# Wider fill matmuls, gated second halves and gated loads in a fused Sinkhorn-attention and bilinear FFN kernel

## The chip, the cores and the metric

The kernel runs on one core of a Trainium2 chip. The metric is the device time of one execution in microseconds (us); for the kernel before, it is the median of 11 runs. The engines are named TensorE (PE in the profile, its weight loads PEld), VectorE (DVE), ScalarE (ACT), GpSimd (POOL) and SyncE (SP). In this kernel POOL issues all loads from DRAM (they cast fp32 to bf16 on the way), and SP issues everything else: DMA transposes, a round trip of v through DRAM, and the stores.

## The reference

Inputs are q, k, v of shape (4, 8, 768, 64), a sort matrix of 8x8 for each batch and head, and three weights.

```python
P = sort_net
for _ in range(5):
    P = P - np.max(P, axis=-1, keepdims=True)
    P = np.exp(P)
    P = P / (np.sum(P, axis=-1, keepdims=True) + 1e-09)
    P = P / (np.sum(P, axis=-2, keepdims=True) + 1e-09)
k_sorted = np.einsum('bhij,bhjcd->bhicd', P, k_b).reshape(B, H, S, D)
v_sorted = np.einsum('bhij,bhjcd->bhicd', P, v_b).reshape(B, H, S, D)
...
scores = scale * np.matmul(q_b, k_sb.transpose(0, 1, 2, 4, 3))
...
attn = attn / (np.sum(attn, axis=-1, keepdims=True) + 1e-09)
return np.matmul(attn, v_sb).reshape(B, H, S, D).astype(np.float32)
```

The keys and values of the 8 blocks (96 tokens each) are mixed by P, each block of queries attends to its own mixed block, and the result x, as 3072 tokens of 512, goes through `(x @ w_a) * (x @ w_b) @ w_out` with 1536 hidden columns.

## The kernel before

**Tiling and stages.** The four batches are worked in order; the 8 heads of a batch are four pairs p, and a pair's 8 blocks are two halves h of four. One unit of attention is (b, p, h): the mixing matmuls of k and v with the spread P (L496 for batch 0, where each half is mixed by itself; L485 and L533 later), a transpose of v (L555, not for batches 2 and 3), scores (L574), exp on ACT (L579), the product with v (L589), and on DVE a reciprocal and a multiplication into xp (L595, L600; the operation `o_mul`). Then x is transposed into xT: batch 0 by TensorE (L608) and a copy, later batches by a DMA transpose on SP (`x_dma`, L616). q is transposed by TensorE for batches 0 and 1 (L469) and by a DMA transpose on SP for batches 2 and 3 (`q_dma`, L621; `QDMA`, L194). For batches 2 and 3 v goes through DRAM and comes back in another layout (`v_out` L542, `v_back` L546).

After a batch's attention come the two FFN stages. Batch 0 has plain products (`ab_plain`, L743; half t of the tokens needs xT of all four pairs' half h = t). Batches 1 to 3 use a Strassen scheme (`ab_strassen`, L825) on sums that `x_sums` and `w_sums` make (L306, which is the line of every two-operand elementwise operation). In it each column group g has two chains of 14 matmuls; ACT takes snapshots (L834), DVE adds (a and f), and DVE or POOL multiplies the two results into hT. `out_plain` (L893) does the last product; the attention of batch b+2 is mixed into `out_plain` of batch b.

**What sets the order.** No loop order is written out. Each piece of work is an `Op` with an engine (or alternatives with a duration each), a duration in the plan's own us, what it depends on (`deps`), which buffers it takes and gives back (`get`, `put`), and a rank. `Plan.solve` (L132) runs a list schedule: at each step it takes the operation that can start earliest, the lowest rank among those that can start within a small margin, on the engine that ends it first. Every engine and every DMA queue then runs its instructions in the order of the planned starts, so an instruction that waits holds up all behind it on its engine. Latencies after an operation are `LAT` or the `lat` given.

**Loads.** `load` (L311) puts an issue of 0.72 on POOL and a transfer on a planned DMA queue. A load waits for the one seven before it (`ld_n[-7]`), and for its buffer: the rings k2, v2 and q2 have 6 buffers each, for 16 pairs in all. `load_pair` (L394) loads k, v and q of a pair; for batches 2 and 3 q is loaded by `q_wide` (L350) in two DMAs. The loads of batches 2 and 3 are added one after the other at L941 to L943 with ranks 30 to 43, with no dependency other than buffers and the seven.

**Batch 0.** L921 to L927 add the first halves of the four pairs at ranks 0 to 3, L929 to L935 the second halves at ranks 10 to 25, which depend only on their loads and buffers. `ab_plain` of batch 0 has ranks from 10.

**Fill.** While TensorE has nothing to do in the first 32.6 planned us (`warm_until`, L973), `_fill` (L177) adds matmuls whose result nobody reads, so that TensorE is not idle. `warm` (L967) writes them to a PSUM bank of their own, n matmuls of 128 columns per planned gap:

```python
unit = 0.056 if t > 4.0 else 0.08
n = int((o.start - t - 0.05) / unit)
```

Of the kernel before, what the change touches and what calls it, by code (L numbers as in the profile page):

```python
# [35 lines left out]
class Plan:  # L36
# [12 lines left out]
    def add(self, eng, dur, fn, deps=(), get=(), put=(), rank=0.0, lat=None):  # L49
        alts = dict(eng) if isinstance(eng, (list, tuple)) else {eng: dur}  # L50
        op = Op(alts, fn, deps, list(get), list(put), rank, lat, len(self.ops))
        for key in op.put:
            self.holders[key] = self.holders.get(key, 0) + 1
        self.ops.append(op)
        return op
# [121 lines left out]
    def _fill(self):  # L177

        t, ops = self.warm_from, sorted((o for o in self.ops if o.eng == "PE"), key=lambda o: o.start)
        for o in ops:  # L180
            if o.start > self.warm_until:
                break
            unit = 0.056 if t > 4.0 else 0.08
            n = int((o.start - t - 0.05) / unit)
            if n > 1:
                w = Op({"PE": 0.0}, lambda n=n: self.warm_fn(n), [], [], [], 0.0, None, -1)
                w.eng, w.start, w.end = "PE", t, t + n * unit
                self.ops.append(w)
            t = max(t, o.end)

# [8 lines left out]
def kernel(  # L199
# [11 lines left out]
    nc = tc.nc  # L211
    P = 128
    B, H, S, D = q.shape
# [9 lines left out]
    HP = H // 2  # L223
# [16 lines left out]
    add = plan.add  # L240
# [3 lines left out]
    ps = [psp.tile([P, 2, 512], FP32, name=f"ps{n}") for n in range(4)]  # L244
# [64 lines left out]
    ld_n = []  # L309

    def load(fn, nbytes, deps=(), get=(), rank=0.0, many=0.0):  # L311
        ds = list(deps) + ([ld_n[-7]] if len(ld_n) >= 7 else [])
        i = add("POOL", 0.72 + many, fn, ds, get=get, rank=rank, lat=0.0)
        d = add("DQ", nbytes / 333e3, None, [i], rank=rank)
        ld_n.append(d)
        return d
# [33 lines left out]
    def q_wide(b, p):  # L350
        t = buf(("q2", b, p))
        for e in range(2):
            nc.gpsimd.dma_start(  # L353
                out=_ap(t, e * D, [[2 * W, P], [2 * D, NCH], [1, D]]),
                in_=_ap(q, (b * H + 2 * p + e) * S * D, [[W, P], [D, NCH], [1, D]]))

    def kv(b, p, name, t):
        nc.gpsimd.dma_start(  # L358
            out=buf((name, b, p)),
            in_=_ap(t, (b * H + 2 * p) * S * D, [[W, P], [S * D, 2], [1, W]]))  # L360
# [30 lines left out]
    for c in range(1, 4):  # L391
        load_ab(c)

    def load_pair(b, p, rank):  # L394
        for name, t, into in (("k2", k, k_in), ("v2", v, v_in)):
            into[b, p] = load(lambda name=name, t=t: kv(b, p, name, t), NB_KV,
                              get=[(name, (name, b, p))], rank=rank)
        if QDMA(b, p):
            q_in[b, p] = load(lambda: q_wide(b, p), NB_KV * 1.5,
                              get=[("q2", ("q2", b, p))], rank=rank, many=0.9)  # L400
        else:
            q_in[b, p] = load(lambda: nc.gpsimd.dma_start(
                out=buf(("q2", b, p)),
                in_=_ap(q, (b * H + 2 * p) * S * D, [[W, P], [S * D, 2], [1, W]])), NB_KV,
                get=[("q2", ("q2", b, p))], rank=rank)


    last = o_p
# [54 lines left out]
    def q_pe(b, p, h):  # L463
        q2, ps_ = buf(("q2", b, p)), buf(("qp", b, p, h)).bitcast(BF16)
        i0, n = (0, NB) if h is None else (h * NBH, NBH)
        p0, np_ = i0 * CG, n * CG
        for c in range(NCH):
            for e in range(2):
                nc.tensor.matmul(  # L469
                    ps_[e * D:(e + 1) * D, c * np_:(c + 1) * np_],  # L470
                    lhsT=_ap(q2, p0 * 2 * W + e * W + c * D, [[2 * W, np_], [1, D]]),
                    rhs=ident[p0:p0 + np_, p0:p0 + np_], is_transpose=True)
# [31 lines left out]
                           [[2 * HK, P], [CG, NCH], [BLK, NBH], [1, CG]]),  # L504
             _ap(buf((what + "m", b, p, h)), 0, [[1024, P], [n, NCH], [CG, NBH], [1, CG]]))

    def mix_half(b, p, what, h, rk):
        pe = add("PE", 0.3, lambda: mix_half_pe(b, p, what, h),
                 [(k_in if what == "k" else v_in)[b, p], s_ok[b, p]],
                 get=[("bank", (what + "m", b, p, h))], put=[(what + "2", b, p)], rank=rk)  # L510
        op = add((("ACT", 0.48), ("DVE", 0.56)), None, None,
                 [pe, o_pads, first.get((what + "T", b, p))],
                 get=[(what + "T", (what + "T", b, p))] if h == 0 else [],
                 put=[(what + "m", b, p, h)], rank=rk)
        first[what + "T", b, p] = op
        op.fn = lambda: mix_half_copy(op.eng, b, p, what, h)
        return op
# [97 lines left out]
    def x_dma(b, p):  # L615
        nc.sync.dma_start_transpose(  # L616
            out=_ap(buf(("xT", b)), p * S, [[KA * S, P], [BLK, NB], [1, BLK]]),
            in_=buf(("xp", b, p)).rearrange("q i e d -> q (i e d)"))

    def q_dma(b, p):  # L620
        nc.sync.dma_start_transpose(  # L621
            out=_ap(buf(("qT", b, p)), 0, [[NB * BLK, P], [P, NCH], [1, P]]),
            in_=buf(("q2", b, p)))
# [33 lines left out]

    first = {}

    def q_part(b, p, h, rk):  # L660
        if QDMA(b, p):
            return add("SP", 1.2, lambda: q_dma(b, p), [q_in[b, p]], get=[("qT", ("qT", b, p))],
                       put=[("q2", b, p)], rank=rk, lat=2.6)
        qi = q_in[b, p, h] if (b, p, h) in q_in else q_in[b, p]
        pe = add("PE", 0.38 if h is not None else 0.46, lambda: q_pe(b, p, h), [qi, o_ident],
                 get=[("bank", ("qp", b, p, h))], put=[("q2", b, p)], rank=rk)
        alts = (("ACT", 0.48),) if h == 0 else (("ACT", 0.48), ("DVE", 0.36)) if h == 1 else (
            ("ACT", 0.8), ("DVE", 0.55))
        op = add(alts, None, None, [pe, first.get(("q", b, p))],
                 get=[("qT", ("qT", b, p))] if h in (0, None) else [],  # L670
                 put=[("qp", b, p, h)], rank=rk)
        first["q", b, p] = op
        op.fn = lambda: q_copy(op.eng, b, p, h)
        return op
# [28 lines left out]
    def x_home(b):  # L703
        if ("xTgot", b) not in st:
            st["xTgot", b] = add("NIL", 0.0, None, get=[("xT", ("xT", b))], rank=-20)
        return st["xTgot", b]
# [9 lines left out]
    def attention(b, p, rk):  # L716
        qd = q_part(b, p, None, rk)
        ks, vs = mix_part(b, p, rk, False)
        if not VDMA(b, p):
            vs = [v_part(b, p, None, vs[0], rk)]  # L720
        ms = [so_part(b, p, h, False, ks[0], qd, vs[0], rk + 0.5 + 0.1 * h) for h in range(2)]
        d = add("SP", 1.2, lambda: x_dma(b, p), ms + [x_home(b)], put=[("xp", b, p)],
                rank=rk + 0.7, lat=2.6)
        for h in range(2):
            xT_done.setdefault((b, h), []).append(d)
# [195 lines left out]
    for p in range(HP):  # L921
        rk = float(p)
        qd = q_part(0, p, 0, rk)
        kd = mix_half(0, p, "k", 0, rk)
        vd = v_part(0, p, 0, mix_half(0, p, "v", 0, rk + 0.05), rk + 0.1)
        m = so_part(0, p, 0, True, kd, qd, vd, rk + 0.1)
        x_part(0, p, 0, m, rk + 0.15)  # L927
    R0 = 10.0
    for p in range(HP):  # L929
        rk = R0 + 5.0 * p  # L930
        qd = q_part(0, p, 1, rk)
        kd = mix_half(0, p, "k", 1, rk)
        vd = v_part(0, p, 1, mix_half(0, p, "v", 1, rk), rk + 1.0)
        m = so_part(0, p, 1, True, kd, qd, vd, rk + 1.0)
        x_part(0, p, 1, m, rk + 2.0)  # L935
    for p in range(HP):
# [1 line left out]
    later_spreads(5)  # L938
    for c in range(3):
        load_out(c, 20)  # L940
    for b in range(2, B):  # L941
        for p in range(HP):
            load_pair(b, p, 30 + 10 * (b - 2) + p)  # L943

    for t in range(2):
        for m in range(KO):
# [6 lines left out]
    for b in range(B):  # L953
        for t in range(2):
            for c in range(3):
                out_plain(b, t, c, RB + 40.0)
        if b + 1 == B:
            break
        if b + 2 < B:
            for p in range(HP):  # L960
                attention(b + 2, p, RB + 36.0 + 0.5 * p)
        tx_ok = x_sums(b + 1, RB + 49.0)
        for g in range(G):
            ab_strassen(b + 1, g, RB + 50.0 + 4 * g, ws_ok, tx_ok, out_last[b])
        RB += 100.0

    def warm(n):  # L967
        touched.add(7)
        for _ in range(n):
            nc.tensor.matmul(ps[3][:, 1, 0:P], lhsT=warm_sb[:, 0:P], rhs=warm_sb[:, 0:P],  # L970
                             start=True, stop=True)

    plan.warm_until, plan.warm_fn, plan.warm_from = 32.6, warm, 1.2  # L973
    order = plan.solve()
# [74 lines left out]
```

## Time and profile before

| what | value |
|---|---|
| median of 11 runs | 257.68 us (254.27 to 259.05) |
| the profiled execution's own time | 257.37 us |
| its span, first to last instruction | 255.6 us |
| mean granted TensorE clock | 0.963 of full |
| TensorE busy | 237.2 us (93%), 2322 matmuls, 2335 weight loads |
| VectorE, ScalarE, GpSimd busy | 158.0, 124.3, 100.6 us |
| software DMA queue (POOL's loads) | 29296 packets, 14.16 MB, 45.2% of 16 engines' span |
| hardware DMA queue (SP's) | 27312 packets, 13.38 MB, 27.1% |
| instruction queue | 18 packets, 0.29 MB |

How to read it: times are counted from the span's start. A row of slices cuts the span in 40 equal parts, and each digit is a busy share in tenths; PEclk is the TensorE clock that was granted. A wait is the idle time of an engine before an instruction, with what ended it; "issue" is idle time for which the profile shows nothing that was waited for. The chain of waits is followed back from the last instruction, at each step to what released it. A line L306 or L248 is a helper's, so such groups are told apart by their tiles.

### The profile page before, as it was taken

The numbers are of one execution on the slowest core, as the hardware profiler recorded it, in microseconds if no ns is written. First come the engines' busy times: TensorE is split into PE (matmuls) and PEld (weight loads), VectorE is DVE, ScalarE is ACT, GpSimd is POOL, SyncE is SP. The second block draws the span as 40 slices with busy tenths as digits, with TensorE's granted clock in tenths as the row PEclk, the third lists the DMA queues.
The fourth block names the chain that finished last, engine by engine and source line by source line (L and its number), as shares of the span: only waits on it lengthen the run. The fifth ranks groups of instructions, "written<-read, shape, count | busy, mean of one in ns | idle before, by whom it ended". The sixth has DMA issues, their size and how long they took to land.

```text
span 255.6 us, 5986 instructions
## 1 busy us (share of the span) xinstructions
PE 237.2 (93%) x2322; PEld 144.0 (56%) x2335; DVE 158.0 (62%) x363; ACT 124.3 (49%) x240; POOL 100.6 (39%) x122
## 2 busy tenths in 40 slices
PE   8987999999999943999999999999999999999992
PEld 7865875666665412455565445556564455655440
DVE  6664589945566305558897646678895329888120
ACT  3353645466765522246667543476661136765010
POOL 8879936843945700002434320044440002455000
PEclk9996599999999995999999999999999999999998
DMA  5999992999999999974003476310024451000135
GB/s 75 170 201 188 204 201 37 170 191 193 161 148 184 166 123 190 253 169 92 0 1 61 95 181 165 80 44 0 0 43 83 94 121 35 1 0 3 41 82 123
DMA packets 56636, 27.91 MB, mean 109 GB/s; under 512 B 36641, under 2 KB 53537, under 8 KB 56609
## 3 DMA queue, kind: packets, MB, share of 16 engines
q0 software_dynamic: 29296, 14.16, 45.2%
q1 hardware_dynamic: 27312, 13.38, 27.1%
q8 instruction: 18, 0.29, 0.5%
q14 instruction: 10, 0.07, 0.1%
HBM read 29.89 MB, written 7.86 MB: 148 GB/s over the span
## 4 chain that ended last, share of the span: by engine, by line
PE 86%; DMA 7%; issue 2%; POOL 2%; ACT 1%; DVE 1%; DVEq 0%
PE ps L825 32%; PE ps L893 23%; PE ps L743 12%; DMA qT<-q 5%; PE ps L589 4%; PE ps L574 3%; PE ps L485 3%; DMA q<-in_q_dram 2%; PE ps L555 2%; PE ps L496 2%; PE ps L970 2%; PE ps L469 2%; PE ps L533 1%; PE ps L608 1%; POOL k L358 1%
## 5 line engine op out<-in xcount | busy, mean ns | idle before, releaser
L306 POOL TENSOR_TENSOR hT<-a,f 128x384 bf16<-128x384 bf16 x39 | 35.5, 917 | 107.1 <-DVE f L306 104.0
L893 PE MATMUL ps<-w_out_sb,hT 128*128 128x512 bf16 x275 | 64.2, 380 | 1.1 <-issue 0.7
L834 ACT COPY f<-ps 128x384 f32<-128x384 f32 x108 | 48.2, 482 | 21.4 <-PE ps L825 18.0
L893 PEld LDWEIGHTS <-hT 128*128 128x128 bf16 x288 | 27.3, 98 | 30.9 <-issue 0.5
L579 ACT ACTIVATE eT<-ps 96x768 bf16<-96x768 f32 x32 | 25.1, 805 | 30.0 <-PE ps L574 29.6
L306 DVE TENSOR_TENSOR f<-f,ps 128x384 f32<-128x384 f32 x54 | 29.2, 549 | 7.4 <-PE ps L825 5.3
L306 DVE TENSOR_TENSOR a<-f,ps 128x384 bf16<-128x384 f32 x54 | 29.6, 549 | 5.2 <-ACT f L834 3.7
L306 DVE TENSOR_TENSOR hT<-a,ps 128x384 bf16<-128x384 bf16 x42 | 23.0, 547 | 6.5 <-PE ps L743 3.4
L248 ACT COPY o<-ps 128x512 f32<-128x512 f32 x13 | 7.5, 585 | 36.5 <-PE ps L893 33.7
L825 PE MATMUL ps<-tx,ws_b 128*128 128x384 bf16 x108 | 24.9, 326 | 0.0
L825 PE MATMUL ps<-tx,ws_a 128*128 128x384 bf16 x108 | 24.0, 326 | 0.0
L600 DVE TENSOR_TENSOR xp<-ps,rec 96x512 bf16<-96x512 f32 x32 | 21.6, 682 | 0.4
L250 DVE COPY o<-ps 128x512 f32<-128x512 f32 x11 | 7.6, 687 | 20.3 <-PE ps L893 20.2
L743 PE MATMUL ps<-xT,w_a_sb 128*128 128x384 bf16 x96 | 19.6, 326 | 0.0
L743 PE MATMUL ps<-xT,w_b_sb 128*128 128x384 bf16 x96 | 19.6, 326 | 0.0
L825 PEld LDWEIGHTS <-ws_b 128*128 128x128 bf16 x144 | 14.1, 98 | 9.4
L825 PEld LDWEIGHTS <-ws_a 128*128 128x128 bf16 x144 | 13.6, 98 | 10.0 <-ACT f L834 0.6
L749 ACT CAST a<-ps 128x384 bf16<-128x384 f32 x24 | 11.4, 477 | 14.2 <-PE ps L743 11.7
L574 PE MATMUL ps<-qT,kT 64*128 64x96 bf16 x256 | 10.4, 213 | 7.8 <-DMA qT<-q 7.7
L825 PE MATMUL ps<-xT,w_a_sb 128*128 128x384 bf16 x72 | 17.6, 326 | 0.0
L825 PE MATMUL ps<-xT,w_b_sb 128*128 128x384 bf16 x72 | 17.6, 326 | 0.0
L353 POOL DMA_DIRECT2D q<-in_q_dram x16 | 13.2, 830 | 5.9 <-DMA k<-in_k_dram 2.7
(92 smaller groups left out, 338.7 us busy)
## 6 DMA issues: line engine op xcount, KB each, us to landing
out_dram<-o SPq DMA_DIRECT2D x48, 128.0 KB, 2.4
k<-in_k_dram POOLq DMA_DIRECT2D x16, 192.0 KB, 6.7
v<-in_v_dram POOLq DMA_DIRECT2D x16, 192.0 KB, 7.2
q<-in_q_dram POOLq DMA_DIRECT2D x24, 96.0 KB, 8.3
w_a_sb<-in_moe_w_a_dram POOLq DMA_DIRECT2D x4, 384.0 KB, 7.8
w_b_sb<-in_moe_w_b_dram POOLq DMA_DIRECT2D x4, 384.0 KB, 9.5
w_out_sb<-in_moe_w_out_dram POOLq DMA_DIRECT2D x3, 512.0 KB, 11.2
vd<-vm SPq DMA_DIRECT2D x8, 192.0 KB, 2.8
```

The source lines that it names most:

```text
L306: ENG[eng].tensor_tensor(out=out, in0=in0, in1=in1, op=op)
L353: nc.gpsimd.dma_start(out=_ap(t, e * D, [[2 * W, P], [2 * D, NCH], [1, D]]), in_=_ap(q, (b * H + 2 * p + e) * S * D, [[W, P], [D, NCH], [1 ...
L485: nc.tensor.matmul(mix[e * D:(e + 1) * D, c // 4, c % 4 * P:(c % 4 + 1) * P], lhsT=src[:, e, c * D:(c + 1) * D], rhs=s_all[:, b * H + 2 * ...
L574: nc.tensor.matmul(sc[:, e, i * BLK:(i + 1) * BLK], lhsT=kT[e * D:(e + 1) * D, at:at + P], rhs=rhs, start=True, stop=True)
L579: nc.scalar.activation(out=buf(("eT", b, p, h))[:, :, 0:HB], in_=buf(("sc", b, p, h))[0:BLK, :, 0:HB], func=AF.Exp, scale=float(scale))
L589: nc.tensor.matmul(ops_[:, e, i * OW:(i + 1) * OW], lhsT=eT[:, e, i * BLK:i * BLK + P], rhs=vs[:, h * NBH + i, e * OW:(e + 1) * OW], start ...
L600: nc.vector.tensor_tensor(out=_ap(xp, h * NBH * 2 * D, [[NB * 2 * D, BLK], [D, 2], [2 * D, NBH], [1, D]]), in0=_ap(ops_, 2, [[1024, BLK], ...
L743: nc.tensor.matmul(pf[:, 0:HW], lhsT=w_sb[:, kc, m * P:(m + 1) * P], rhs=buf(("xT", b))[:, kc, t * HW:(t + 1) * HW], start=(kc == 0), stop ...
L749: ea = add("ACT", 0.48, lambda: nc.scalar.copy(out=buf(("a", b, t, m)), in_=buf(("pf", b, t, m, "a"))[:, 0:HW]), [pa], get=[("a", ("a", b, ...
L825: nc.tensor.matmul(buf(key)[:, 0:HW], lhsT=lf(j), rhs=rf(j), start=start and j == 0, stop=j == 1, skip_group_check=not start)
L834: return add("ACT", 0.48, lambda: nc.scalar.copy(out=buf((name, b, g, n)), in_=buf(kA)[:, 0:HW]), [dep], get=[("f", (name, b, g, n))], rank=r)
L893: nc.tensor.matmul(po, lhsT=hT[:, t * 2 + m // G, m % G, c * P:(c + 1) * P], rhs=w_out_sb[:, m, :], start=(m == 0), stop=(m == KO - 1), sk ...
```

## The change

It has four parts.

1. Fill: the gap is counted in columns, not matmuls, and `warm` makes matmuls of 512 columns and one rest of at least 32. Up to 5 planned us the rate is 1180 columns per us, later 2350. They write the whole of the same PSUM bank.
2. Batch 0: the q, k and v matmuls of a pair's second half get a dependency on the `o_mul` of the same pair's first half (`st["gate", p]`).
3. Loads: only batch 2 is loaded where batches 2 and 3 were. The loads of batch 3 are added after the attention of batch 2, at ranks 40 to 43, and each k, v and q load depends on `o_mul` of batch 2, pair 2, second half (`st["last", 2, 2]`).
4. Plan: `q_dma` counts 1.3 us with 3.2 until it has landed (before 1.2 and 2.6), `x_dma` 1.5 (before 1.2).

```diff
-            unit = 0.056 if t > 4.0 else 0.08
-            n = int((o.start - t - 0.05) / unit)
-            if n > 1:
-                w = Op({"PE": 0.0}, lambda n=n: self.warm_fn(n), [], [], [], 0.0, None, -1)
-                w.eng, w.start, w.end = "PE", t, t + n * unit
+            rate = 2350.0 if t > 5.0 else 1180.0
+            cols = int((o.start - t - 0.06) * rate)
+            if cols >= 64:
+                w = Op({"PE": 0.0}, lambda cols=cols: self.warm_fn(cols), [], [], [], 0.0, None, -1)
+                w.eng, w.start, w.end = "PE", t, t + cols / rate
...
-        ds = list(deps) + ([ld_n[-7]] if len(ld_n) >= 7 else [])
+        ds = [d for d in deps if d is not None] + ([ld_n[-7]] if len(ld_n) >= 7 else [])
...
-    def load_pair(b, p, rank):
+    def load_pair(b, p, rank, after=None):
         for name, t, into in (("k2", k, k_in), ("v2", v, v_in)):
-            into[b, p] = load(lambda name=name, t=t: kv(b, p, name, t), NB_KV,
+            into[b, p] = load(lambda name=name, t=t: kv(b, p, name, t), NB_KV, [after],
...
-            q_in[b, p] = load(lambda: q_wide(b, p), NB_KV * 1.5,
+            q_in[b, p] = load(lambda: q_wide(b, p), NB_KV * 1.5, [after],
...
-    def mix_half(b, p, what, h, rk):
+    def mix_half(b, p, what, h, rk, after=None):
         pe = add("PE", 0.3, lambda: mix_half_pe(b, p, what, h),
-                 [(k_in if what == "k" else v_in)[b, p], s_ok[b, p]],
+                 [(k_in if what == "k" else v_in)[b, p], s_ok[b, p], after],
...
-    def q_part(b, p, h, rk):
+    def q_part(b, p, h, rk, after=None):
         if QDMA(b, p):
-            return add("SP", 1.2, lambda: q_dma(b, p), [q_in[b, p]], get=[("qT", ("qT", b, p))],
-                       put=[("q2", b, p)], rank=rk, lat=2.6)
+            st["q", b, p] = add("SP", 1.3, lambda: q_dma(b, p), [q_in[b, p]],
+                                get=[("qT", ("qT", b, p))], put=[("q2", b, p)], rank=rk, lat=3.2)
+            return st["q", b, p]
...
-        pe = add("PE", 0.38 if h is not None else 0.46, lambda: q_pe(b, p, h), [qi, o_ident],
+        pe = add("PE", 0.38 if h is not None else 0.46, lambda: q_pe(b, p, h), [qi, o_ident, after],
...
-        d = add("SP", 1.2, lambda: x_dma(b, p), ms + [x_home(b)], put=[("xp", b, p)],
+        st["last", b, p] = ms[1]
+        d = add("SP", 1.5, lambda: x_dma(b, p), ms + [x_home(b)], put=[("xp", b, p)],
...
+        st["last", p] = m
     R0 = 10.0
     for p in range(HP):
+        st["gate", p] = st["last", p]
+    for p in range(HP):
         rk = R0 + 5.0 * p
-        qd = q_part(0, p, 1, rk)
-        kd = mix_half(0, p, "k", 1, rk)
-        vd = v_part(0, p, 1, mix_half(0, p, "v", 1, rk), rk + 1.0)
+        go = st["gate", p]
+        qd = q_part(0, p, 1, rk, go)
+        kd = mix_half(0, p, "k", 1, rk, go)
+        vd = v_part(0, p, 1, mix_half(0, p, "v", 1, rk, go), rk + 1.0)
...
-    for b in range(2, B):
-        for p in range(HP):
-            load_pair(b, p, 30 + 10 * (b - 2) + p)
+    for p in range(HP):
+        load_pair(2, p, 30 + p)
...
+            if b + 3 < B:
+                for p in range(HP):
+                    load_pair(b + 3, p, 40 + p, st["last", b + 2, 2])
...
-    def warm(n):
+    def warm(cols):
         touched.add(7)
-        for _ in range(n):
-            nc.tensor.matmul(ps[3][:, 1, 0:P], lhsT=warm_sb[:, 0:P], rhs=warm_sb[:, 0:P],
+        while cols >= 32:
+            n = min(cols, 512)
+            nc.tensor.matmul(ps[3][:, 1, 0:n], lhsT=warm_sb[:, 0:P], rhs=warm_sb[:, 0:n],
                              start=True, stop=True)
+            cols -= n
```

## The prediction

> **What bounds the kernel now.** The page first: TensorE is busy for 237.2 of 255.6 us, so time can only come from its idle stretches, from a lowered clock, and from work that serves nothing. The slices show where to look.
>
> ```profile
> PE   8987999999999943999999999999999999999992
> PEclk9996599999999995999999999999999999999998
> DMA  5999992999999999974003476310024451000135
> ```
>
> One slice is 6.39 us. TensorE has one deep hole (slices 14 and 15, 90 to 102 us), and the granted clock falls twice: in slices 3 and 4 (19 to 32 us) and in slice 15. The DMA engines are full from 6 to 38 us and again from 45 to 109 us, so both holes lie where a transfer has to queue. Next the list of waits, of which these two are TensorE's large ones:
>
> ```profile
> PE ps L574 <- DMA qT<-q: 7.7, 1, 7.7
> PE ps L589 <- issue: 2.5, 1, 2.5
> ```
>
> Then the chain of waits around the first:
>
> ```profile
> 85.86 2.05 PE ps L893 x9
> 87.91 0.15 issue
> 88.06 0.09 PE ps L574
> 88.16 11.72 DMA qT<-q
> 99.87 0.04 issue
> 99.92 0.51 PE ps L574 x8
> 100.42 0.78 PE ps L485 x12
> 101.20 0.76 PE ps L533 x2
> ```
>
> The q transpose of batch 2, pair 2, is issued on SP's queue at 88.16 and lands at about 99.9. TensorE runs out of other work at 92.27 (TensorE's timeline: 10 matmuls of L893 from 89.93, 2.33 us) and stands for 7.65 us. The DMA answer for 88 to 92 us gives landings of 10.9 us for the two transposes issued there; over the whole run the median is 5.6, the least 2.7, and in 104 to 110 us, with little else on the engines, 4.1. What fills the engines is the last batch's loads, on POOL's timeline:
>
> ```profile
> 81.70 0.70 POOL L358 DMA_DIRECT2D k<-in_k_dram  x1 [2.57 <-PE ps L485]
> 82.40 0.73 POOL L358 DMA_DIRECT2D v<-in_v_dram  x1
> 83.11 1.64 POOL L353 DMA_DIRECT2D q<-in_q_dram  x2
> 85.03 0.70 POOL L358 DMA_DIRECT2D k<-in_k_dram  x1 [0.27 <-PE ps L485]
> 85.72 0.73 POOL L358 DMA_DIRECT2D v<-in_v_dram  x1
> 86.43 1.65 POOL L353 DMA_DIRECT2D q<-in_q_dram  x2
> ```
>
> These are batch 3, pairs 2 and 3 (pairs are counted back from the last load of all). They land 11 to 14 us later (DMA answers for 84 to 92 us), at about 100. That is the time at which qT lands. Batch 3 needs none of it before 140 us, where its first mixing matmuls (L485) stand in the chain.
>
> The second hole has no wait behind it; from the chain:
>
> ```profile
> 17.59 0.50 PE ps L496 x24
> 18.09 0.20 PE ps L589 x3
> 18.29 2.51 issue
> 20.80 0.32 PE ps L589 x5
> ```
>
> It cuts a group of eight matmuls in the middle. I read it as instruction fetch. The page has 18 packets of 16 KB in the instruction queue, and TensorE 4,657 instructions: 259 for each. In the quiet part of the trace, from 121 us, these packets start 244 to 267 TensorE instructions apart, each near instruction 256k-64. Instruction 3x256-64 = 704 is where TensorE stops at 18.29, and the packet that it lacks starts at 18.4 (DMA answer for 18 to 19 us). The page before it began at instruction 448, at 14.78 us: 256 instructions ran in 3.5 us, while a fetch through full DMA engines took 6.0 us (14.78 to 20.80).
>
> **The change, part by part. Loads of batch 3 gated.** Nothing of the 12 loads (16 transfers) goes away. They wait for o_mul of batch 2, pair 2, second half, the sixth o_mul of that batch, which ends at 111.6 (DVE's timeline), so they leave the stretch from 69 to 104 us. Removed: 7.65 us of standing, and the cold clock after it. That I price row by row against the same groups when warm: L574 0.51 and 0.43 against 0.28 twice, L485 0.78 against 0.46, L533 0.76 against 0.43, one L893 0.63 against 0.22, ten L893 2.35 against 2.16: 1.6 us. Together 9.3. What remains: with 88.16 as the issue time the transpose lands at 90.9 (2.7), 92.3 (4.1) or 93.8 (5.6), and TensorE comes for it at 92.27: 0, 0 or 1.5 us. The engines are then as in the 4.1 row; I take 0.5. So -8.8, with ends -9.3 and -5.
>
> The new place costs something. 8 issues at 0.72 and 8 at 0.83 are 12.4 us of POOL, from about 101 (111.6 less what is gained by then), and the four q transposes behind them on SP. Behind them on POOL stand the products hT of the next stage, which starts at 113.1 before. In its first 11 us POOL did five of them (116.91, 120.40, 122.5 twice, 124.47); moved to VectorE at 0.55 us they make 2.75 us of work where VectorE has 1.04+0.66 us free in 113 to 123. So 0 to 1 us late, and TensorE waits only if the a and f buffers run out: +0.5. The Trainium skill speaks against the move too ("DMA: Bandwidth & Descriptors", SWDGE vs HWDGE vs iDMA): GpSimd's descriptor rings lie in SBUF, and VectorE's two-port modes lock GpSimd out of it. The row for it: loads at 42 to 46 us, with VectorE busy 4.82 of 5 us, took 0.72 to 0.76 us each to issue; at 85 to 88, with VectorE at 1.55 of 4, 0.70 to 0.73. If it doubled the issue time, an estimate, POOL would lose 12.4 us more; the rows add 0.3. I take the rows. For the end of the loads: 101+12.4+7 = 120, transposed by 126; the scores need them at 142.2 less 10, 132. Covered by 6 us.
>
> **Wide fill.** The same columns in a quarter of the matmuls. All fill up to 14.4 us hides under the Sinkhorn chain (ACT and VectorE until p_rep at 12.9), so its own time is worth nothing. The first fill's planned rate drops to 1180 columns per us, so it ends before the q transposes of 6.14: also nothing. What could count is the fetch. By the trace 163 fill matmuls lie before 14.45 (59, 23, 45, 33, 3). From n=(gap-0.05)/unit I get the gaps back, and cols=(gap-0.06)*rate makes 11, 6, 12, 9, 1 = 39. A weight load goes with each, so 248 instructions vanish: a page less 8. So the page that began at 14.78 becomes the first that is fetched, again at about 14.75, in the same matmuls, through the same full engines; it arrives again near 20.8, and TensorE again has 256 instructions to spend. The stall stays, 2 to 2.5 us. The skill ("Runtime: NRT & Kernel Launch", Instruction fetch mechanics) has fetch in 16 KiB blocks hidden by slow dispatch; the row shows 2.5 us that are not hidden. By the rule there is no fetch stall for this edit to touch; by the row there is one and it stays. Both give 0; if the count is off by a third of a page, the row gives up to -2.5, and -3.7 for the clock that falls with it (groups at 21.5 to 31.7 us at half clock: L496 12 in 0.46 against 0.25, L555 4 in 0.54 against 0.28 and so on, 3.7 in all).
>
> **Second halves gated.** No work is removed; the q, k and v matmuls of a pair's second half wait for the first half's o_mul (pair 0: 22.15). Behind them TensorE's order is replanned, so first halves end together. Today the last of them is transposed (L608) at 35.30, and the first dense product (L743) starts at 35.47. Three more exps at 0.8 after 21.9, then L589, o_mul, L608 and copy would put it at about 27. The gain is not the 8 us: TensorE is full from 20.80 to 35.47, and the second halves' work comes later instead. The gain is the holes that L970 plugs there, 0.33+0.64+0.39+0.50+0.34 = 2.2 us, since L743 can fill them. Against it: dense 384-column matmuls run at half clock until 31.7 if it recovers no sooner, +0.7 beyond what small ones lose. Net -1.5, ends +1 and -3.5. The gate also holds the k2 and q2 buffers longer, which loads of batch 1, pair 2, need; these go out at 42.3 and the DMA share is 0.20 in 40 to 45, so that is covered. **Costs in the plan** (1.3, 3.2, 1.5 for SP's transposes) move instructions in the order only: 0, within 1 either way.
>
> **Sum.** -8.8+0.5-1.5 = -9.8. The profiled execution took 257.37 (span 255.60 and 1.77 around it): 247.6. The median of 11 is 0.31 above it: 247.9.
>
> **Rivals.** (B) The fetch stall and the cold stretch after it go as well: -6.2 more, 241.7. For: the page count is near a boundary[...]. Against: the count above. (C) The transpose stays late without the loads: four xT transposes (issued 80.53 to 86.38) stand before it on SP and may be the slow part; their landings of 7 to 10 us were under the same load. Residue 4 to 5 us: 252.5. (D) Gain eaten by waits of the new order: about 257. (E) Slower: SP's order puts batch 3's q transposes behind the xT transposes of batch 2, which wait for the end of Strassen products (136.9 before, some 126 after, 7.3 us to issue). Then qT comes at 126+7.3+4.1 = 137 where 132 is needed, and each later one 3.4 behind (the issue time at 88): up to 12 us with the clock, 260. It decides from the point at which qT of batch 3 lands 10 us late. Against: on today's queue they stand before xT (106 to 116).
>
> **How the numbers follow.** A 0.58 (245.5 to 250.5), B 0.12, C 0.14, D 0.07, E 0.09. The prediction is A. The range 241.5 to 254.5 takes in A, B and C and leaves D and E out. Over 1% (2.6 us, what can be told from no change here) faster: A, B, C, rounded to 0.82; same 0.08; slower 0.10.
>
> **What would show it.** Right: no wait of L574 for qT above 2 us, full clock after 32 us, batch 3's loads on POOL after 95; a hole marked issue of 2 to 2.5 us near 18 to 21 still there; L743 from about 27 and hardly any L970 after 21. Wrong: qT landings over 7 us near 90, a wait of L574 or L485 after 125, or VectorE late on a and f in the first Strassen stage.

## The result and the profile after

| kernel | median | ratio to before (95% interval) | span of the profiled execution |
|---|---|---|---|
| before | 257.79 us (47 runs) | 1 | 255.6 |
| after | 252.63 us (12 runs) | 0.984 (0.980 to 0.988) | 249.6 |

The change makes the kernel 1.6% faster where 3.8% was forecast. 252.63 lies within the stated range and near rival C (252.5), but the forecast of 247.9 promised about twice the gain. Each of these kernels has some executions that are a few per cent longer at a lower granted clock; the medians take in all executions and the ratios leave those out, so a ratio need not be that of the two medians.

The slices of the page after show what went and what came:

```profile
PE   7998996999999998589999999999999999999992
PEclk9999999999999999799999999999999999999999
DMA  5999998999993799999003487300064450000135
```

The half clock near 20 us is gone. A hole and a lowered clock are still there, in slices 15 and 16 (counted from 0; 94 to 106 us), and the DMA engines are still full in slices 14 to 18. Two rows of the list of waits name the hole:

```profile
POOL tx L306 <- DMA xT<-xp: 19.1, 1, 19.1
PE ps L589 <- DMA vs<-vd: 4.1, 2, 2.9
```

TensorE no longer waits for qT; that wait has left the list. It now waits for vs, twice, at 99.35 and at 105.71 on its timeline:

```profile
102.25 1.04 PE L589 MATMUL ps<-vs,eT 96*128 96x66 bf16 x16 [2.90 <-DMA vs<-vd]
106.91 0.42 PE L589 MATMUL ps<-vs,eT 96*128 96x66 bf16 x8 [1.20 <-DMA vs<-vd]
```

The first is v of pair 2, sent back by SP at 94.74; the second is v of pair 3, on which the chain of waits runs:

```profile
90.06 0.97 DVE vm L250
91.03 0.02 issue
91.05 7.41 DMA vd<-vm
98.46 0.02 issue
98.48 8.39 DMA vs<-vd
106.87 0.04 issue
106.91 0.42 PE ps L589 x8
```

v of batch 2, pair 3, goes out to DRAM in 7.4 us and comes back in 8.4, where the least of this trace is 3.2 for the second leg; pair 2's came back in 7.5. What may slow both stands on POOL's timeline:

```profile
85.83 1.63 POOL L306 TENSOR_TENSOR tx<-xT,tx 128x768 bf16<-128x768 bf16 x1 [19.14 <-DMA xT<-xp]
87.42 0.74 POOL L358 DMA_DIRECT2D k<-in_k_dram  x1
88.16 0.72 POOL L358 DMA_DIRECT2D v<-in_v_dram  x1
88.87 1.65 POOL L353 DMA_DIRECT2D q<-in_q_dram  x2
```

These are batch 3's first loads. The sixth o_mul of batch 2, which they were to wait for, ends at 106.0 on VectorE's timeline:

```profile
105.34 0.68 DVE L600 TENSOR_TENSOR xp<-ps,rec 96x512 bf16<-96x512 f32 x1
```

So the loads start 18.6 us before their gate, and the last of the 16 transfers is issued at 104.4. What seems to have held them until 87 (tested below) is the line above them: a sum tx that the new plan put on POOL and that waits for xT. The code agrees. `emit` turns a dependency of the plan into a wait only for instructions of TensorE, ACT and DVE (`engines`, L982 before; and of these only for work on PSUM), and a load is issued on POOL. For a load the plan's dependency, the one on the load seven before it too, sets the place in POOL's order and nothing else.

The first 35 us: the stall in the matmul groups is still there, but short.

```profile
19.00 0.15 PE ps L496
19.15 0.77 issue
19.92 0.38 PE ps L496 x11
```

### The profile page after: what moved, and what is told of

Its sections match the earlier page's. It is cut to its first block, busy times and chain, and to the rows that moved or that the text cites. A ratio compares the mean times of both kernels' runs of the same rounds, so it can differ in the third digit from the quotient of the medians.

```text
span 249.6 us, 5707 instructions
## 1 busy us (share of the span) xinstructions
PE 234.6 (94%) x2177; PEld 133.6 (54%) x2192; DVE 158.2 (63%) x359; ACT 125.8 (50%) x243; POOL 102.4 (41%) x123
## 4 chain that ended last, share of the span: by engine, by line
PE 81%; DMA 9%; issue 3%; DVE 3%; ACT 1%; POOL 1%; SPq 0%; ACTq 0%; DVEq 0%
PE ps L827 33%; PE ps L895 20%; PE ps L745 11%; DMA vs<-vd 3%; DMA vd<-vm 3%; PE ps L574 3%; PE ps L485 3%; PE ps L979 2%; PE ps L589 2%; PE ps L496 2%; DMA q<-in_q_dram 2%; PE ps L555 2%; PE ps L469 1%; PE ps L533 1%; DMA out_dram<-o 1%
## 5 line engine op out<-in xcount | busy, mean ns | idle before, releaser
L895 PE MATMUL ps<-w_out_sb,hT 128*128 128x512 bf16 x276 | 64.5, 381 | 0.8 <-issue 0.3
L895 PEld LDWEIGHTS <-hT 128*128 128x128 bf16 x288 | 27.1, 98 | 30.9 <-ACT o L248 0.4
L248 ACT COPY o<-ps 128x512 f32<-128x512 f32 x12 | 7.0, 586 | 37.0 <-PE ps L895 28.8
L827 PE MATMUL ps<-tx,ws_a 128*128 128x384 bf16 x108 | 24.9, 326 | 0.0
L827 PE MATMUL ps<-tx,ws_b 128*128 128x384 bf16 x108 | 24.8, 326 | 0.0
L250 DVE COPY o<-ps 128x512 f32<-128x512 f32 x12 | 8.3, 688 | 24.9 <-PE ps L895 22.1
L745 PE MATMUL ps<-xT,w_b_sb 128*128 128x384 bf16 x96 | 19.6, 327 | 1.2 <-DVE hT L306 1.2
L745 PE MATMUL ps<-xT,w_a_sb 128*128 128x384 bf16 x96 | 19.6, 327 | 0.0
L827 PEld LDWEIGHTS <-ws_b 128*128 128x128 bf16 x144 | 14.0, 98 | 9.8 <-ACT f L836 0.3
L827 PEld LDWEIGHTS <-ws_a 128*128 128x128 bf16 x144 | 13.7, 98 | 9.1 <-ACT f L836 0.4
L827 PE MATMUL ps<-xT,w_a_sb 128*128 128x384 bf16 x72 | 18.0, 332 | 0.0
L827 PE MATMUL ps<-xT,w_b_sb 128*128 128x384 bf16 x72 | 17.6, 326 | 0.1
L589 PE MATMUL ps<-vs,eT 96*128 96x66 bf16 x256 | 12.4, 197 | 4.3 <-DMA vs<-vd 4.1
```

Source lines behind the costliest of these rows:

```text
L250: eng.tensor_copy(out=out, in_=in_)
L589: nc.tensor.matmul(ops_[:, e, i * OW:(i + 1) * OW], lhsT=eT[:, e, i * BLK:i * BLK + P], rhs=vs[:, h * NBH + i, e * OW:(e + 1) * OW], start ...
L745: nc.tensor.matmul(pf[:, 0:HW], lhsT=w_sb[:, kc, m * P:(m + 1) * P], rhs=buf(("xT", b))[:, kc, t * HW:(t + 1) * HW], start=(kc == 0), stop ...
L827: nc.tensor.matmul(buf(key)[:, 0:HW], lhsT=lf(j), rhs=rf(j), start=start and j == 0, stop=j == 1, skip_group_check=not start)
L895: nc.tensor.matmul(po, lhsT=hT[:, t * 2 + m // G, m % G, c * P:(c + 1) * P], rhs=w_out_sb[:, m, :], start=(m == 0), stop=(m == KO - 1), sk ...
```

## The experiments

The theory after the result: the loads were moved, not gated; they left the stretch in which qT is fetched and now fill the one in which v makes its round trip. The rival: v's trip is late for reasons of its own (SP's order, two transfers in series). A second question was what became of the fetch stall. In the table, each kernel is named by its run, "first part" is the start of the last L743-type product of batch 0 with w_b, and "rest" is the span less that.

| kernel | median | ratio to before (95% interval) | first part | rest |
|---|---|---|---|---|
| before | 257.79 | | 80.6 | 175.0 |
| after | 252.63 | 0.984 (0.980 to 0.988) | 77.3 | 172.3 |
| e1_real_gate | 246.80 | 0.954 (0.949 to 0.958) | 77.5 | 166.8 |
| e2_loads_only | 257.36 | 0.998 (0.994 to 1.002) | 78.9 | 176.2 |
| e3_fill_only | 257.27 | 0.992 (0.988 to 0.996) | 78.9 | 175.6 |
| e4_halves_only | 254.91 | 0.982 (0.976 to 0.987) | 79.3 | 173.0 |
| e5_page_shift | 246.35 | 0.956 (0.952 to 0.960) | 77.7 | 166.7 |
| e6_tx_off_pool | 255.36 | 0.990 (0.985 to 0.994) | 77.6 | 177.5 |
| e7_before_real_gate | 249.24 | 0.966 (0.961 to 0.971) | 80.6 | 166.1 |
| e8_sums_later | 245.82 | 0.952 (0.948 to 0.957) | 76.0 | 167.7 |

### A gate that holds

```diff
...
+                held = add("POOL", 0.1, lambda: nc.gpsimd.tensor_copy(
+                    out=held_sb, in_=buf(("xp", 2, 2))[:, NB - 1, 1, 0:2]),
+                    [st["last", 2, 2]], put=[("xp", 2, 2)], rank=39)
                 for p in range(HP):
-                    load_pair(b + 3, p, 40 + p, st["last", b + 2, 2])
+                    load_pair(b + 3, p, 40 + p, held)
```

> The changed kernel, but a small copy on POOL that reads what o_mul of batch 2, pair 2, second half wrote stands ahead of batch 3's loads, so they cannot start before it. Theory (the gate of the change is only in the plan; POOL goes on to the loads as soon as it is free, at 87 us, and they slow v's round trip through DRAM): TensorE's two waits for vs, 2.9 and 1.2 us, go, and with them the 3.4 us of half clock (about 1.5 us): 252.6 - 5.6 = 247.0, no hole over 1 us between 90 and 110 us. Rival (vs is late because of SP's order and its own two trips, not the loads): 252 to 253 and both waits stay. Second rival (loads now come too late for batch 3): a wait of L485 or L574 after 125 us, over 253.

Measured: 246.80 us. On POOL's timeline the copy stands 14.6 us for o_mul, and the loads follow:

```profile
102.21 0.18 POOL L969 COPY held_sb<-xp 96x2 bf16<-96x2 bf16 x1 [14.57 <-DVE xp L601]
102.71 0.74 POOL L359 DMA_DIRECT2D k<-in_k_dram  x1 [0.32 <-PE ps L828]
103.44 0.73 POOL L359 DMA_DIRECT2D v<-in_v_dram  x1
104.15 1.65 POOL L354 DMA_DIRECT2D q<-in_q_dram  x2
```

The DMA answers set the two kernels side by side, vd as issued in 88 to 92 us and vs as issued in 92 to 96; first after, then this one:

```profile
vd<-vm SPq DMA_DIRECT2D x2, 192.0 KB, 6.7
vs<-vd SPq DMA_DIRECT2D x1, 192.0 KB, 7.5
```

```profile
vd<-vm SPq DMA_DIRECT2D x2, 192.0 KB, 2.4
vs<-vd SPq DMA_DIRECT2D x2, 192.0 KB, 3.0
```

The same kinds of transfer, in the same order on SP, land in less than half the time. (In this kernel pair 3's vs also goes out before 96, hence x2.) Both waits for vs are gone, the clock is full until the last slice, and TensorE has no hole over 0.2 us after 43 us. So the rival falls: SP's order was not what made v late. Nor do the loads come too late for batch 3, though they run into the Strassen stage and occupy POOL until 116.5. This is the kernel that the prediction described, and it takes 246.8 where 247.9 was forecast.

The same copy put into the kernel before, with the loads and nothing else moved:

> The kernel before with batch 3's loads behind a copy on POOL that reads o_mul's output, and nothing else changed. Theory: both the wait for qT (7.65 us) and the waits for vs are gone, with their cold clock: 257.8 - 9.3 + 0.5 = 249.0; the hole of 2 to 2.5 us near 18 us stays. Rival (the gated second halves or the fill have a part in what the real gate gave): 251 to 254.

Measured: 249.24. The rest fell from 175.0 to 166.1, by 8.9, and the stall of 2.48 us at 18.3 stays. The loads behind a real gate are thus worth 3.4% by themselves, twice the whole change.

### The loads moved in the plan alone, and what held them

```diff
...
-    for b in range(2, B):
-        for p in range(HP):
-            load_pair(b, p, 30 + 10 * (b - 2) + p)
+    for p in range(HP):
+        load_pair(2, p, 30 + p)
...
+            if b + 3 < B:
+                for p in range(HP):
+                    load_pair(b + 3, p, 40 + p, st["last", b + 2, 2])
```

> The kernel before with the third part alone: batch 3's loads added behind batch 2's attention, with the dependency in the plan. Theory: the wait of 7.65 us for qT and its cold clock (1.6) go, and waits for vs of about 4.1 us with 1.5 of cold clock come in their place: 257.8 - 3.7 = 254.1. The fetch stall of 2.5 us near 18 us stays. Rival (the gain of the change came from the first 35 us): 257 to 258.

Measured: 257.36, no difference that can be told. The mechanism is as expected and its size is not. The wait for qT is gone, and waits for vs stand in its place:

```profile
PE ps L589 <- DMA vs<-vd: 7.0, 2, 4.7
```

7.0 us and two stretches of 3.4 us at half clock (from 102.6 and 112.8) against 7.65 and one of 6.8: one stall was exchanged for another of the same price. It is worse here than in the change. The first wait is 4.71 us against 2.90: TensorE ran out of other work 1.10 earlier (98.25), and pair 2's v came 0.71 later (102.96). The second is 2.28 against 1.20, and there SP's queue has pair 2's vs ahead of pair 3's vd (96.01 and 96.43), so the two trips run one after the other, while in the change vd of pair 3 goes out at 91.05, before vs of pair 2 (94.74). Which of the change's other edits reordered them was not separated.

The next run takes away the instruction that held the loads at 87 us, by letting only VectorE do the sums tx:

```diff
     def x_sums(b, rank):
 
-        al = (("DVE", 0.55), ("POOL", 1.75))
+        al = (("DVE", 0.55),)
```

> The changed kernel with its gate in the plan, but the token sums tx only on VectorE, so that no instruction of POOL that waits for xT stands ahead of batch 3's loads. Theory (the loads are held back by that tx alone): the loads start at about 67 us as in the kernel before, run until 85, and the large wait for qT or for vs is back, 5 to 8 us with its cold clock: 252.6 + 2 = 255. Rival (some other wait holds the loads): they still start at 87, 252 to 253.

Measured: 255.36. Batch 3's first load goes out at 67.24, with nothing in front of it, and TensorE stands 8.47 us for vs at 92.8:

```profile
67.24 0.72 POOL L358 DMA_DIRECT2D k<-in_k_dram  x1
68.27 0.72 POOL L358 DMA_DIRECT2D v<-in_v_dram  x1 [0.31 <-PE ps L574]
```

So in the changed kernel the loads are held by the accident that one tx landed on POOL.

### The fill and the second halves alone

Fill alone (the first hunk and the last of the change's diff):

> The kernel before with the fill alone changed. Theory (fetch in pages of 256 instructions; the first page crossing lands at instruction 192, in the q transposes at 14.7 us, and the page runs out at instruction 448, in the o matmuls at 18.1): the stall stays at 1.8 to 2.6 us near 18 us, half clock follows, 257.8 within 1. Rival (fewer instructions free the fetch): no stall, no half clock, 252 to 254.

Measured: 257.27, with the hole of 2.45 us at 18.12. Making the fill of a quarter as many matmuls does not free the fetch, as the count of instructions had said. The 0.8% may be the clock: half clock lasts 3.4 us here after the hole and 10.2 in the kernel before. But e2 has the old fill and the old order up to there, and it too shows 3.4 us; so the length of the half clock is not the fill's doing alone, and one profile of each cannot give any part of it to the fill.

Second halves alone (`after` in `mix_half` and `q_part`, `st["gate", p]`):

> The kernel before with the gate of the second halves alone, narrow fill kept. Theory: the fetch stall is still there, but in a stretch where TensorE has fewer instructions ready, so 1 to 2 us; first L743 at 27 to 29 us instead of 35.3; 257.8 - 2 = 255.8. Rival (the gate alone makes all of the change's early gain): 254.5. Second rival (it needs the wide fill): 257.8.

Measured: 254.91. The hole is 1.11 us at 19.87 and the first L743 starts at 28.6. The expectation was right for this part. In this build the wait for qT has also become one for vs (4.4 us), though the code of the loads was not touched. On its POOL timeline a tx that waits for xT stands among batch 3's loads (90.06), and those of pair 3 go out behind it, from 93.66: the new order of the plan made the same accident here. Its rest is 2.0 us shorter for that.

Its first part, 79.3, contains a stretch of half clock that the changed kernel's does not have (43.3 to 46.7 us, behind two waits for hT). Priced against the rows of the change at full clock it costs 1.4 us: L496 0.53 against 0.38 and 0.51 against 0.36, L743 1.46 against 0.82, L608 0.53 against 0.34, L574 0.50 against 0.34, L555 0.53 against 0.39. Without it the first part would be 77.9, where the change has 77.3. So most of the gain in the first part comes from the gated second halves.

### Fetch pages

The real gate, with the first fill group in 128 columns: 66 more TensorE instructions (matmuls and their weight loads), order otherwise the same.

```diff
...
     def warm(cols):
+        wide = 128 if 7 not in warmed else 512
+        warmed.add(7)
         touched.add(7)
         while cols >= 32:
-            n = min(cols, 512)
+            n = min(cols, wide)
```

> The real gate, and the first fill group in 128 columns again: 66 more TensorE instructions with nothing else in the order changed. Theory (pages of 256): the first crossing moves from 14.5 to about 11.5 us, its page is there by 17, before the 256 instructions in hand run out at about 17.8; the next crossing is then at 17.8 and in time too. The hole of 0.8 to 0.9 us near 19.5 us goes, by adding instructions: 246.8 - 0.8 = 246.0. Rival (the hole has to do with how many fill matmuls there are, or with what runs there): it stays or grows, 246.8 or more.

Measured: 246.35, against 246.80, which the intervals do not tell apart. The hole near 19.6 is gone, as expected: the first instruction packet starts at 15.1 (18.1 in e1), and L497 runs on through 19.06 to 19.4. But another hole stands later, which was not expected:

```profile
28.14 0.09 PE ps L609 x2
28.23 1.52 issue
29.75 0.26 PE ps L609 x2
```

It too cuts a group of four in the middle, and the third packet starts at 27.5, too late by as much. Adding instructions moves the hole, so it is a matter of where the page edges fall, and not of fewer fill matmuls being better.

The other traces agree. With all instructions of TensorE and its sequencer counted, the hole comes after 447 or 448 of them (after, e1, e3, e6, e8), after 705 (before, e2, e4, e7) or after 958 (e5): within two of points that lie 256 apart. And in all ten it ends 2.2 to 2.5 us after a packet of the instruction queue starts (before: 18.41 and 20.80).

### Weight sums later

In the change (and in e1) TensorE stands 1.21 us at 39.7 and 0.74 at 42.0 for VectorE's hT, behind ws in the chain of waits (34.62 ws_b 0.85, 40.84 ws_a 0.54).

```diff
...
-                    dj = d + ([oks
+                    dj = d + h_done[0, 1, 0] + ([oks
```

> The real gate, and the weight sums ws made to wait in the plan until the first dense product of the second half of batch 0 is done. Theory (the two waits for VectorE's hT at 40 to 43 us, 1.95 us together, come from ws crowding VectorE while the second halves run too): both go, 246.8 - 1.9 = 244.9. Rival (VectorE is late there because of the second halves alone): they stay, 246 to 247; second rival (the later sums crowd the attention of batch 1): waits of 1 to 2 us between 55 and 75, 247 to 248.

Measured: 245.82. Both waits are gone and the first part is 1.5 us shorter, of which 0.9 comes back in the rest. This is the fastest kernel of the study, though the interval does not part it from e1.

## Why the prediction was wrong

**Loads of batch 3 gated: the step that failed.** The prediction said of the loads: "They wait for o_mul of batch 2, pair 2, second half". They do not. The dependency is only the plan's, and POOL ran on to them at 87.42; the prediction's own sign was loads after 95. The term was -8.8+0.5 = -8.3 us; the rest fell by 175.0-172.3 = 2.7. The holes account for most of the difference: 2.90+1.20 us for vs, and 1.4 us of half clock behind them, from rows priced as in the prediction (L589 1.04 against 0.67, which is the same row in e1; L574 0.50 against 0.34, L895 1.03 against 0.59, L827 0.84 against 0.49, L574 0.45 against 0.34), together 5.5. The 0.1 left was not traced. Where the wait is real, the term comes out: -8.2 in e1, -8.9 in e7.

The price itself was right in its parts. qT of batch 2, pair 2, is issued at 83.77 after and no wait follows it. The prediction took its landing from the row of 4.1; the landings in 84 to 88 us are 3.2. The prediction priced two places for the loads, the old one and the one behind the gate, and not the one between, where they went (87 to 104 us). There they met v's trip, whose two legs stand in the page's issue list. Behind a real gate they do not meet it (e1), so the overlap with v follows from the failed step and is not a second one.

**The cost at the new place** was put at +0.5. In the changed kernel the loads never came there; in e1, where they did, it is not seen: POOL issues loads until 116.5 and does three hT in a row after that, VectorE is busy 4.68 of 5 us in 104 to 109, and TensorE 5.00 of 5 in the windows from 104 to 118. Nor did rival E's order come about: SP issues batch 3's four q transposes from 108.99 and the xT transposes behind them from 125.78. The rule of the Trainium skill on VectorE locking GpSimd out of the descriptor rings ("DMA: Bandwidth & Descriptors", SWDGE vs HWDGE vs iDMA) is not seen at work either: loads beside that VectorE took 0.72 to 0.75 us to issue, as elsewhere. The page says it of VectorE's two-port modes; whether VectorE was in one there, the trace does not show.

**Wide fill.** "The stall stays, 2 to 2.5 us" is right for the fill alone (2.45 us, e3). In the whole change it is 0.77. The prediction's count placed the page edges with the old order of work. With second halves held back, the 256 instructions in hand run out at 19.15 instead of 18.29, and this time the page came at 19.92 instead of 20.80. No half clock follows it. In the ten profiles none follows a stall of 0.60 to 1.52 us, and one follows each of 1.73 to 2.51. So part of rival B came true, through the gated second halves and not through the fill.

**Second halves gated.** Forecast -1.5 (ends +1 and -3.5) with the first L743 at about 27; it starts at 27.9, and the first part is 3.3 us shorter. Clock and fetch, which the prediction had given to the fill's own term, are in these 3.3, and 1.95 us of new waits for hT (see e8) have already been taken off. Part of the 3.3 is not the gate's: e2 and e3, with second halves as before, end the first part at 78.9 in their profiles, with a shorter half clock. Against those the change gains 1.6, about what was forecast.

**Costs in the plan** were put at 0; they were not run alone.

**Sum.** -2.7-3.3 = -6.0 us of span; -9.8 was forecast, and the gate that holds gives 257.9-246.8 = 11.1 by the medians, with the loads' term as forecast (8.2 in the profile) and a first part that gained 3.1 where 1.5 was forecast. Of the rivals, C has the number (252.5) with another cause: nothing remained of the wait for qT, it went to the next transfer in line. That is D's mechanism, at half its price. So it is luck that the result lies in the stated range, next to C's number.

## What to carry to other kernels

A dependency in a planner orders instructions; it holds an engine only if it becomes a wait. Before pricing a gate, find in the code the line that emits the wait for that engine, above all for engines that only issue transfers.

When a block of transfers is moved, list every other transfer that the critical path needs in the old stretch and in the new one. Here the loads left qT and met vd and vs, and the moved part alone was worth nothing.

Count instructions to the page edge with the order that the change will give, not with the old one.

## What the runs showed of the hardware

In the kernel before, with the DMA engines full, a TensorE page of 256 instructions took 6.0 us from the page edge before it to its own first instruction (14.78 to 20.80), and the 256 instructions in hand, small matmuls and their weight loads, ran in 3.5 us; so TensorE stood for 2.5. 66 added instructions removed a hole of 0.87 us and opened one of 1.52.

The half clock that follows the hole near 18 us lasted 10.2 us in the profiled executions of the kernel before (hole of 2.51 us) and of e7 (2.48), and 3.4 in those of e3 (2.45) and e2 (1.73, with the same work up to there); the length of the hole alone does not set it. The first part then ends at 80.6 or at 78.9. In e4, 3.4 us of half clock follow two waits for hT of 1.21 and 0.74 us; in after and e1 the same two waits are followed by none. Some of the spread of the kernel before (254 to 260 us) may come from this; it was not tested.

Loads on POOL's queue delayed SP's transfers: the way of v to DRAM took 2.4 us without them (e1) and 6.7 beside them (after), the way back 3.0 and 7.5.
